# Decode attention with its gradients: scores of chunk pairs through four 32-column array tiles, a first load moved ahead, and another row order for one weight

## The chip, the core and the metric

The kernel runs on one core of one Trainium2 chip. The metric is the time on the device in microseconds (us); the median of a kernel's runs is quoted.

## What is computed

One decode step of an attention layer plus a gated MLP, forward and all gradients, in bf16. The caches of 32 heads hold 8192 positions of 128 values each; there is one query.

```python
def _A_ref(x, k_cache, v_cache, wq, wo):              # x: [1, 1, 640]; k_cache, v_cache: [1, 32, 8192, 128]
    q = (x @ wq).reshape(B, Sq, Hq, Dh) ...
    scores = jnp.einsum("bhqd,bhkd->bhqk", q, k) * (Dh ** -0.5)
    p = softmax(scores)
    o = jnp.einsum("bhqk,bhkd->bhqd", p, v)
    return o.reshape(B, Sq, Hq * Dh) @ wo
def _B_ref(x, w1, w3, w2):                            # w1, w3: [640, 1728]; w2: [1728, 640]
    return (silu(x @ w1) * (x @ w3)) @ w2
out = x + _A_ref(layernorm(x), ...) + _B_ref(layernorm(x), ...)
# outputs: out, and the gradients of x, k_cache, v_cache, wq, wo, w1, w3, w2 for a given grad_out
```

The gradient of the K cache is an outer product per head (a weight per position times q), that of the V cache another (the probabilities times dO, the gradient of the head's output). So each head loads K and V, 2 MB each, and stores dK and dV, 2 MB each: 64 loads and 64 stores of 2 MB make up 134 MB each of the 151.67 MB read and the 151.34 MB written.

## The kernel before

Positions lie on the 128 partitions, 64 per partition. A ring of ten slots of 2 MB holds the caches; a head's gradients are written over its caches and stored from the same slot, and when the store has been issued the next load waits for a slot to become free. The MLP runs once, just before head 2, in four of the ten slots. The parts that matter here (cuts marked):

```python
    load_group(0, nc.sync)                     # wq and wo of the first four heads, rows of 1 KB and 1280 B
    for _ in range(4):
        load_next()                            # K0, V0, K1, V1
    # ... slots for the MLP; w2a is 12 blocks of 128 rows of w2
    fifo(w2a, B_w2[0:NBA * P, :].rearrange("(fb p) c -> p fb c", p=P))      # pieces of 1280 B
    # ...
    def T(h, kind, c):                         # one of eight chunks of a head's K or V
        W3 = kv_tiles[(kind, h)][:].bitcast(F32)...            # a pair of bf16 is moved as one fp32
        pT = pst()                             # one of four PSUM tiles
        for k in range(4):
            nc.tensor.transpose(pT[:, k * P:(k + 1) * P], W3[:, 4 * c + k, :], ident_f[:])
        KT = kt_tile()                         # one of four copy tiles in SBUF
        nc.scalar.copy(KT..., pT[:])
    def M(h, kind, c):                         # scores (K) or V*dO (V) of the chunk: 8 matmuls
        # ...
        for k in range(4):
            for par in range(2):
                nc.tensor.matmul(S_[kind][:, 0:J], lhsT=KTb[:, k, par, :], rhs=S_["cz"][:, o:o + J], ...)   # J = 64
    def wsum(h, kind, pair):                   # weighted sum over the positions, in four column tiles
        nc.tensor.matmul(X[:], lhsT=zeros, rhs=W[:, 0:N4], start=True, ...)     # clears the tile
        for i in range(J // 4):
            q = QW * (i % 4)                   # QW = 32
            nc.tensor.matmul(X[q:q + 4, :], lhsT=pair[:, 4 * i:4 * i + 4, 0], rhs=W[:, N4 * i:N4 * (i + 1)], ...)
        nc.scalar.copy(XS..., X[:])
    # ... MLP
            nc.tensor.matmul(gu_ps[0:rows, wi, b:b + 1], lhsT=wrow(wi, ci)[:, b * P:b * P + rows], ...)
            # ...
            nc.scalar.copy(bc_sb[:, wi, f0:f1], pb[:, 0:f1 - f0])
    # ... after a head's dK: store("K", h), which issues the store and then load_next()
```

A head has two long products per cache on VectorE (the gradients), 16 chunks of transposes with 16 copies on ScalarE, 128 score matmuls and four groups of small sums on TensorE.

## Time and profile before

| | before |
|---|---|
| time, median of the runs beside the changed kernel (six) | 743.96 us (743.29 to 746.13) |
| bytes moved over the span | 304.3 MB in 743.1 us |
| TensorE, VectorE, ScalarE busy | 82%, 60%, 50% |
| a head that never waits for a load, from row maximum to row maximum | 17.6 to 18.1 us |
| a head on average (heads 3 to 31) | 20.69 us |

Lines of the page. The row "DMA" is the busy share of the 16 DMA engines in 40 slices of the span, in tenths; "GB/s" what they moved. A group line reads: line, engine, operation, output<-input, shapes, count | busy us, mean ns | idle time of the engine before it, and what ended most of that.

```profile
span 743.1 us, 20151 instructions
...
PE 607.7 (82%) x8767; PEld 512.8 (69%) x8767; DVE 447.5 (60%) x740; ACT 370.9 (50%) x732; POOL 30.4 (4%) x45
...
DMA  8999999999999999999999999999999999999992
GB/s 320 384 408 419 422 425 428 352 428 421 406 424 431 425 423 427 426 427 426 424 428 426 428 426 425 426 427 426 424 427 426 420 424 423 418 423 421 421 404 92
...
q8 instruction: 69, 1.13, 0.6%
...
DMA 61%; PE 28%; DVE 6%; issue 1%; ACT 1%; SPq 0%; DVEq 0%; ACTq 0%
...
L279 PE MATMUL pT<-ident_f,kv 128*128 128x128 f32 x2048 | 338.9, 291 | 73.9 <-DMA kv<-in_A_k_cache_dram 65.4
...
L298 PE MATMUL dA<-cz,KT 128*128 128x64 bf16 x2048 | 107.7, 197 | 6.6 <-ACT qd L315 4.5
L298 PE MATMUL sA<-cz,KT 128*128 128x64 bf16 x2048 | 102.8, 193 | 0.0
...
L321 DVE TENSOR_REDUCE mrow<-sA 128x1 f32<-128x64 f32 x32 | 7.2, 224 | 60.1 <-PE sA L298 60.1
...
```

What to see: the DMA row is full from the second slice to the last but one, mostly at about 425 GB/s; the chain that ended last is 61% DMA; TensorE's one large idle time, 73.9 us before the transposes of line 279, ended with a K load 65.4 us of the time. The score matmuls of line 298 keep TensorE busy for 107.7 + 102.8 = 210.5 us, but that is hidden: compute waits for transfers. Two blemishes stand in the GB/s row: the eighth slice (352) and the two ends.

The ends, in a table of stretches (start:end, length, then busy us and instructions per engine, granted clock, DMA share, GB/s):

```profile
...
core 0: us, PE busy (x) PEld busy (x) DVE busy (x) ACT busy (x) POOL busy (x), PEclk, DMA share, GB/s
0.00:5.00 5.00, 0.00 (x0) 0.00 (x0) 1.76 (x13) 1.28 (x1) 0.69 (x6) 1.00 0.49 76
...
130.00:150.00 20.00, 19.70 (x313) 17.38 (x311) 14.18 (x20) 12.97 (x26) 0.76 (x1) 1.00 0.93 357
200.00:690.00 490.00, 418.78 (x5964) 353.65 (x5964) 291.73 (x451) 260.82 (x515) 16.31 (x20) 0.92 1.01 425
...
```

In the first 5 us only 76 GB/s flowed; in 130 to 150 us the DMA share was 0.93. The transfers of the last 55 us, in 40 slices of 1.375 us, look like this:

```profile
...
GB/s 441 426 444 432 417 417 441 411 429 441 393 298 477 405 411 334 381 429 405 417 465 429 417 359 407 278 365 267 141 18 30 30 18 27 36 24 24 12 0 0
...
```

Read the last third of that row. Up to about 730 us the engines move hundreds of GB/s. Then nine slices carry 12 to 36 GB/s. All 16 engines together move about 425, so one engine is worth some 27: in these 12 us one engine is finishing alone. The page alone hides it, since the DMA share is a mean of 16. I call it the straggler.

### The profile page before, as it was taken

What the parts mean: (1) busy time and instruction counts of PE and PEld (TensorE: products, weight loads), DVE (VectorE), ACT (ScalarE), POOL (GpSimd) and SP (SyncE); (2) the same over time, 40 slices, a digit from 0 to 9 for tenths busy, and PEclk for the clock granted to TensorE, in tenths of its full rate; (3) what the DMA queues carried; (4) which work ended last, traced back from release to release, by engine and by line L of the source; (5) the groups of instructions that cost most, each with busy time, mean ns of one, the idle gap of its engine ahead of it and who ended that gap; (6) DMA issues with size and microseconds to landing.
All of it is one profiled execution on the core that took longest, in us unless ns stands there. A gap on an engine that the chain in (4) does not pass through costs nothing.

```text
span 743.1 us, 20151 instructions
## 1 busy us (share of the span) xinstructions
PE 607.7 (82%) x8767; PEld 512.8 (69%) x8767; DVE 447.5 (60%) x740; ACT 370.9 (50%) x732; POOL 30.4 (4%) x45
## 2 busy tenths in 40 slices
PE   1997699999998969878797997889698788888920
PEld 1776588888886867767586775767687677777710
DVE  4169927677764745666366664547546666476580
ACT  1651076666664646545365553556455455555510
POOL 0100200000000000001000000000000000000000
PEclk9997799999998999999899998989989999899965
DMA  8999999999999999999999999999999999999992
GB/s 320 384 408 419 422 425 428 352 428 421 406 424 431 425 423 427 426 427 426 424 428 426 428 426 425 426 427 426 424 427 426 420 424 423 418 423 421 421 404 92
DMA packets 29118, 304.32 MB, mean 410 GB/s; under 512 B 2836, under 2 KB 5972, under 8 KB 12644
## 3 DMA queue, kind: packets, MB, share of 16 engines
q1 hardware_dynamic: 22736, 276.39, 88.5%
q0 software_dynamic: 5984, 26.30, 8.8%
q8 instruction: 69, 1.13, 0.6%
q10 hardware_dynamic: 308, 0.33, 0.2%
q14 instruction: 21, 0.17, 0.1%
HBM read 151.67 MB, written 151.34 MB: 408 GB/s over the span
## 4 chain that ended last, share of the span: by engine, by line
DMA 61%; PE 28%; DVE 6%; issue 1%; ACT 1%; SPq 0%; DVEq 0%; ACTq 0%
DMA kv<-in_A_k_cache_dram 27%; DMA out_dram<-kv 26%; PE pT L279 12%; DMA kv<-in_A_v_cache_dram 8%; PE pT L365 3%; PE sA L298 3%; PE dA L298 3%; DVE kv L398 3%; PE hb L391 2%; PE pT L361 1%; PE dh_ps L481 1%; PE hb L377 1%; PE acc L555 1%; PE sA L325 1%; DVE kv L558 1%
## 5 line engine op out<-in xcount | busy, mean ns | idle before, releaser
L281 ACT COPY KT<-pT 128x512 f32<-128x512 f32 x512 | 299.1, 586 | 213.8 <-PE pT L279 187.4
L279 PE MATMUL pT<-ident_f,kv 128*128 128x128 f32 x2048 | 338.9, 291 | 73.9 <-DMA kv<-in_A_k_cache_dram 65.4
L279 PEld LDWEIGHTS pT<-ident_f,kv 128*128 128x128 f32 x2048 | 234.5, 150 | 77.8 <-issue 75.7
L298 PEld LDWEIGHTS <-KT 128*128 128x128 bf16 x4096 | 194.7, 100 | 28.3 <-issue 21.4
L398 DVE TENSOR_TENSOR kv<-qd,U 128x4096 bf16<-128x4096 bf16 x64 | 146.0, 2283 | 0.0
L398 DVE TENSOR_TENSOR kv<-qd,P 128x4096 bf16<-128x4096 bf16 x64 | 143.4, 2282 | 0.0
L298 PE MATMUL dA<-cz,KT 128*128 128x64 bf16 x2048 | 107.7, 197 | 6.6 <-ACT qd L315 4.5
L298 PE MATMUL sA<-cz,KT 128*128 128x64 bf16 x2048 | 102.8, 193 | 0.0
L368 ACT COPY KT<-pT 128x512 f32<-128x512 f32 x64 | 37.5, 586 | 74.0 <-PE pT L365 45.9
L354 DVE SCALAR_TENSOR_TENSOR U<-dA,P 128x64 bf16<-128x64 f32 x32 | 7.4, 232 | 97.1 <-PE dA L298 97.1
L391 PE MATMUL hb<-masks,KT 128*128 128x1 f32 x512 | 65.8, 250 | 0.0
L391 PEld LDWEIGHTS hb<-masks,KT 128*128 128x128 f32 x512 | 62.0, 192 | 0.9 <-issue 0.9
L321 DVE TENSOR_REDUCE mrow<-sA 128x1 f32<-128x64 f32 x32 | 7.2, 224 | 60.1 <-PE sA L298 60.1
L379 DVE SCALAR_TENSOR_TENSOR U<-dA,hb,P 128x128 bf16<-128x128 f32 x32 | 11.4, 355 | 51.0 <-PE hb L377 51.0
L365 PE MATMUL pT<-kv,P 128*4 128x512 bf16 x512 | 41.6, 455 | 0.0
L365 PE MATMUL pT<-kv,U 128*4 128x512 bf16 x512 | 33.1, 379 | 0.4 <-DVE U L379 0.4
L361 PE MATMUL pT<-kv,cz 128*128 128x512 bf16 x64 | 27.6, 432 | 0.0
L448 DVE SCALAR_TENSOR_TENSOR wq_g<-wq_g,side 128x512 bf16<-128x512 bf16 x40 | 27.3, 682 | 0.0
L345 DVE RECIPROCAL rZ<-sA 128x1 f32<-128x1 f32 x32 | 5.4, 168 | 35.7 <-PE sA L339 34.8
L238 DVE SCALAR_TENSOR_TENSOR side<-wo_g,g_bc 128x640 bf16<-128x640 bf16 x32 | 26.1, 817 | 0.3
L365 PEld LDWEIGHTS <-P 128*4 128x4 bf16 x512 | 10.3, 90 | 22.1 <-issue 12.7
L377 PEld LDWEIGHTS hb<-rdot,masks 128*128 128x128 f32 x64 | 11.0, 216 | 17.8 <-issue 17.8
(140 smaller groups left out, 344.7 us busy)
## 6 DMA issues: line engine op xcount, KB each, us to landing
out_dram<-kv SPq DMA_DIRECT2D x64, 2048.0 KB, 31.5
kv<-in_A_k_cache_dram SPq DMA_DIRECT2D x32, 2048.0 KB, 26.7
kv<-in_A_v_cache_dram SPq DMA_DIRECT2D x32, 2048.0 KB, 26.6
out_dram<-wo_g POOLq DMA_DIRECT2D x8, 640.0 KB, 12.2
out_dram<-wq_g POOLq DMA_DIRECT2D x8, 640.0 KB, 13.7
wq_g<-in_A_wq_dram POOLq DMA_DIRECT2D x7, 640.0 KB, 13.7
wo_g<-in_A_wo_dram POOLq DMA_DIRECT2D x7, 640.0 KB, 19.4
kv<-in_B_w_dram SPq DMA_DIRECT2D x2, 1728.0 KB, 16.8
```

Of the source, the lines that this page charges most:

```text
L238: nc.vector.scalar_tensor_tensor(junk[:], G_["wo"][:, hh, :], 1.0, g_bc[:], ALU.mult, ALU.mult, accum_out=G_["do"][:, hh:hh + 1])
L279: nc.tensor.transpose(pT[:, k * P:(k + 1) * P], W3[:, 4 * c + k, :], ident_f[:])
L281: nc.scalar.copy(KT[:].rearrange("p k w -> p (k w)"), pT[:])
L298: nc.tensor.matmul(S_[kind][:, 0:J], lhsT=KTb[:, k, par, :], rhs=S_["cz"][:, o:o + J], start=(i == 0 and par == 0), stop=(par == 1), skip_ ...
L361: nc.tensor.matmul(X[:], lhsT=cz_tiles[0][:, 0:1].to_broadcast([P, P]), rhs=W[:, 0:N4], start=True, stop=False, skip_group_check=True)
L365: nc.tensor.matmul(X[q:q + 4, :], lhsT=pair[:, 4 * i:4 * i + 4, 0], rhs=W[:, N4 * i:N4 * (i + 1)], start=False, stop=(i >= J // 4 - 4), sk ...
L368: nc.scalar.copy(XS[:].rearrange("p k w -> p (k w)"), X[:])
L377: nc.tensor.matmul(S_["hb"][:, 2:3], lhsT=negones_b, rhs=S_["rdot"][:], start=True, stop=True, skip_group_check=True)
L379: nc.vector.scalar_tensor_tensor(S_["U2"][:], S_["V"][:, 0:J].unsqueeze(2).to_broadcast([P, J, 2]), S_["hb"][:, 2:3], S_["P2"][:], ALU.add ...
L391: nc.tensor.matmul(S_["hb"][:, a:a + 1], lhsT=XS[:, r, :], rhs=mask4[:, r:r + 1], start=False, stop=(r == 3), skip_group_check=True)
L398: nc.vector.tensor_tensor(dst[:, lo * DH:hi * DH].rearrange("p (j a b) -> p j a b", a=DH // 2, b=2), vec.rearrange("p (a b) -> p a b", b=2 ...
L448: nc.vector.scalar_tensor_tensor(wq_g[:, ci, :], wq_g[:, ci, :], 1.0, dqb, ALU.mult, ALU.mult, accum_out=dxa[:, ci, g:g + 1])
```

## The change

The intent is to take work off TensorE and to use the transfers better at the start and around the MLP. In scores and V*dO, the chunk was the stationary operand (128 columns) and a 64-column strip moved past it: 8 matmuls per chunk. Now the query strip is stationary (32 columns) and 512 columns of the chunk move; two chunks, each split into even and odd positions, go through four column tiles of the array, so four matmuls serve a pair. The result lies in rows and is turned to columns by a copy and four fp32 matmuls against a 0/1 matrix ("selection"). With it the clearing matmul of the weighted sums goes, K0 is loaded first, w2 is laid out with twelve consecutive rows per partition (15 KB pieces), and the two last small stores are split.

```diff
+    load_next()
     load_group(0, nc.sync)
-    for _ in range(4):
+    for _ in range(3):
         load_next()
...
-    fifo(w2a, B_w2[0:NBA * P, :].rearrange("(fb p) c -> p fb c", p=P))
+    fifo(w2a, B_w2[0:NBA * P, :].rearrange("(p fb) c -> p fb c", fb=NBA))
...
-    def M(h, kind, c):
+    def Mp(h, kind, c0):
...
+        for c in (c0, c0 + 1):
+            KTb = ...
+            for par in range(2):
+                q = QW * (2 * (c - c0) + par)
+                o = QL + QW * (2 * a + par) - c0
+                nc.tensor.matmul(S_[kind][q:q + QW, :], lhsT=S_["qz"][:, o:o + QW], rhs=KTb[:, par, :],
+                                 start=(c0 == 0), stop=(c0 == NCH - 2), skip_group_check=True)
+    def ev(h, kind):
+        XS = kt_tile()
+        nc.scalar.copy(XS[:].rearrange("p k w -> p (k w)"), S_.pop(kind)[:])
+    def selm(h, kind):
         for k in range(4):
-            for par in range(2):
-                nc.tensor.matmul(S_[kind][:, 0:J], lhsT=KTb[:, k, par, :], rhs=S_["cz"][:, o:o + J], ...)
+            nc.tensor.matmul(S_["m"][:, b0:b0 + J]...[:, k, :, :], lhsT=XS[:, k, :], rhs=selc[:]..., ...)
...
     def wsum(h, kind, pair):
-        nc.tensor.matmul(X[:], lhsT=cz_tiles[0][:, 0:1].to_broadcast([P, P]), rhs=W[:, 0:N4], start=True, ...)
...
-                nc.tensor.matmul(gu_ps[0:rows, wi, b:b + 1], lhsT=wrow(wi, ci)[:, b * P:b * P + rows],
+                nc.tensor.matmul(gu_ps[0:rows, wi, b:b + 1], lhsT=fcols(wrow(wi, ci), b, rows),     # every 12th column
...
+                if b0 < NBA:
+                    nc.scalar.copy(bc_sb[:, wi, 0:NBA * P].rearrange("p (f b) -> p b f", b=NBA)[:, b0:b0 + bn, :], ...)
+                    continue
...
-    nc.scalar.dma_start(out_0..., fin_bf[0:NC, :])
-    nc.scalar.dma_start(out_1..., fin_bf[NC:2 * NC, :])
+    for dst, r0, cuts in ((out_0, 0, (0, 3, 5)), (out_1, NC, (0, 4, 5))):
+        for lo, hi in zip(cuts, cuts[1:]):
+            nc.scalar.dma_start(dst...[lo:hi, :], fin_bf[r0 + lo:r0 + hi, :])
```

Left out: the order of the calls in a head, which now treats chunks by pairs; the small sums of a head, which share one PSUM tile ("m") with the turned scores; padding of the probability tiles, with which the weights of each weighted-sum matmul become 32 columns wide instead of 4.

## The prediction

> **What bounds the kernel now.** DMA, and within it one engine. The page counts 304.3 MB over 743.1 us. In the table of stretches the DMA share is 1.0 at 415 to 433 GB/s in almost every 10 us from 10 to 700 us; by the packet records no engine idles except at 0-7 us, 130-148 us (about 1.4 us per engine) and after 700 us. Tensor is 82% busy, but a head that runs freely takes 17.8 us (106.7 to 124.8 to 142.4 us in the chain of waits), its transfers about 20.6 us: compute is hidden.
>
> The end is set by a straggler. The last compute ends at 727 us, fifteen engines finish near 730, yet packets of one engine run on, back to back, until 742 us. In the landings of each 2 MB transfer the sixteenth increment trails the fifteenth by 0.1 us at 190 us, 4 at 390, 9 at 640, 12 to 14 at the end. My reading: instruction fetch. Queue 8 moved 69 packets of 16 KB, 1.01 us each; 17,534 Tensor instructions at 64 B make 68.5 such packets. The Trainium skill, "Runtime: NRT & Kernel Launch", "Instruction fetch mechanics", says instructions are refilled in 16 KiB blocks (256 instructions) by a DMA queue of the sequencer; this trace agrees. The spread between engines at the end (17 to 19 us) fits one engine taking a third of the fetches.
>
> **What the change does.**
> 1. Score matmuls: 4096 of 64 columns become 1024 of 512 in four column tiles. The weighted sums, tiled so already, take 60 ns each (16 in 0.96 us), so a pair of chunks costs about 0.25 instead of 0.8 us. Added: 512 passes of fp32 selection (8 in 0.87 us, as the column sums) and two 0.59 us ScalarE copies per head; 64 zeroing matmuls (0.43 us) go. About -3.5 us of Tensor and +1.2 us of ScalarE per head. Directly worth nothing: off the critical path.
> 2. Tensor instructions fall to about 12,290: 48 fetches instead of 69. With a third on the straggler: about -5.5 us.
> 3. K0 first: from 1 to 7 us the engines moved 0.94 MB in 1 KB pieces where 2.5 MB were possible. 16 KB pieces first hide that: -2 to -3 us. Compute starts about 6 us earlier.
> 4. The hole at 130-148 us comes from late stores after the MLP; earlier, faster heads mostly fill it: -1 us.
> 5. w2a in 15 KB rows instead of 1280 B (61 ns each): -1.3 us. Strided weight loads in the MLP hide under VectorE.
> 6. Split last stores: one of five descriptors sat on the straggler (landing 3.5 to 4.5 us after the others), but the last cache store lands later there: 0.
>
> Sum about -10.5 us. **Predicted 733.5 us, 80% range 728 to 739.** Faster by over 2%: 0.20; within: 0.78; slower: 0.02.
>
> **What would show it.** Queue 8 near 48 packets; DMA share still 1.0 in the plateau; Tensor busy near 500 us, idling more for K and V loads; ScalarE near 405 us; higher GB/s in the first slices and in slice 8 (352 before); lag at the end about 8 us; some 700 packets of 1280 B on queue 1 instead of 2240.
>
> **What would make it wrong.** The straggler has another cause than fetches (about 738); it vanishes and the end falls to the compute tail after the last V load (727 to 730); the ring of copy tiles, now shared by selection, makes a head longer than 20.6 us (slower); Tensor time matters where I call it hidden.

## The result

The changed kernel took 737.50 us (736.41 to 739.99, six runs), the kernel before 743.96 us in the same rounds. The ratio is 0.9914, with a 95% interval of 0.9892 to 0.9936: within 2%, and in the predicted range (728 to 739). The gain is about 6.5 us where 10.5 were predicted. A ratio is computed as the mean time of one kernel's undisturbed runs over that of the other's in the same rounds, so it is not quite the ratio of the medians quoted. All outputs are correct.

The same lines of the page, after:

```profile
span 735.9 us, 14854 instructions
...
PE 639.8 (87%) x6143; PEld 464.7 (63%) x6143; DVE 446.7 (61%) x745; ACT 402.5 (55%) x796; POOL 29.9 (4%) x45
...
DMA  9999999999999999999999999999999999999993
GB/s 338 401 409 421 425 430 423 391 413 410 428 420 423 428 427 426 417 426 428 430 417 425 430 427 426 419 431 425 427 419 427 428 428 429 425 429 429 424 391 150
...
q8 instruction: 48, 0.79, 0.4%
...
PE 64%; DMA 12%; DVE 10%; ACT 8%; issue 3%; ACTq 0%; SPq 0%; DVEq 0%
...
L293 PE MATMUL pT<-ident_f,kv 128*128 128x128 f32 x2048 | 311.3, 291 | 5.9 <-DMA kv<-in_A_k_cache_dram 4.0
...
L328 PE MATMUL m<-selc,KT 128*128 128x16 f32 x512 | 68.0, 265 | 29.3 <-ACT KT L318 29.2
...
L354 DVE TENSOR_REDUCE mrow<-m 128x1 f32<-128x64 f32 x32 | 7.2, 225 | 106.4 <-PE m L328 106.4
...
L312 PE MATMUL sA<-KT,qz 128*32 128x512 bf16 x512 | 56.0, 427 | 0.0
...
L312 PE MATMUL dA<-KT,qz 128*32 128x512 bf16 x512 | 53.6, 404 | 0.2 <-ACT KT L295 0.2
...
```

Instructions fell from 20,151 to 14,854, queue 8 from 69 packets to 48, as predicted, and the score matmuls (line 312 now) are busy for 56.0 + 53.6 = 109.6 us, half of the 210.5 before. What was not predicted: TensorE's busy time rose, from 607.7 to 639.8 us, and the chain that ended last is now 64% TensorE and 12% DMA. The transposes (line 293 now) wait 5.9 us for anything before them, where they waited 73.9. A kernel that waited for transfers now hardly waits. The reason isn't faster transfers: the DMA row is as full as before. The heads have grown by about as much as they used to wait. (The ends of matmuls are modelled in this profile, so the time of a head, below, is a better measure than busy time.) The row maximum shows a longer way within a head: VectorE sat idle before it for 106.4 us in all, 60.1 before; the scores now pass through ScalarE and once more through TensorE (lines 318 and 328) on their way there. The stretches, with the columns as before:

```profile
...
0.00:5.00 5.00, 0.00 (x0) 0.00 (x0) 1.76 (x13) 1.28 (x1) 0.69 (x6) 1.00 0.65 198
...
130.00:150.00 20.00, 18.86 (x187) 13.82 (x186) 12.28 (x18) 11.86 (x25) 0.00 (x0) 0.91 0.99 391
200.00:690.00 490.00, 457.43 (x4370) 328.83 (x4370) 312.26 (x476) 291.76 (x595) 17.95 (x22) 0.94 1.01 426
...
```

The first 5 us carry 198 GB/s, 130 to 150 us carry 391. Over the long plateau from 200 to 690 us, TensorE is busy 457 of 490 us (419 before) and the rate is 426 GB/s (425 before). The end:

```profile
...
GB/s 417 465 441 393 441 453 322 274 322 429 393 435 381 357 381 405 489 429 393 417 405 399 273 367 284 115 24 27 33 30 18 36 0 0 0 0 0 0 0 0
...
```

Six slices, 8 us, below 40 GB/s, where before there were nine.

The heads can be told apart by the reduction in which VectorE takes the row maximum of the scores, one per head:

| us | before | after |
|---|---|---|
| head 1 to head 2, with the MLP between | 55.4 | 63.5 |
| head 2's row maximum at | 100.0 | 111.5 |
| a head that doesn't wait for loads | 17.6 to 18.1 | 19.0 to 20.8 |
| a head, mean of heads 3 to 31 | 20.69 | 20.16 |
| last row maximum at | 700.0 | 696.1 |

### A ledger of DMA engine time

Each DMA packet in the trace has a start, a duration, a size and a queue. Summed and divided by 16, they give the time per engine that transfers took; "idle" is the time in which fewer than 16 packets were under way, times the share of engines missing. (Packet records overlap a little, so the columns add up to some 6 us more than the span, 6.6 before and 6.1 after.) This is worked out from the packet records for the profiled execution of every kernel below (us per engine). "Data" is the time of all packets but the instruction queue's; "fetch" that of the instruction queue; "last" the idle time from 680 us to the end of the last transfer, which is large only if some engine runs on while the others have finished; the two last columns are the part of "data" by which 16 KB packets exceeded their usual 611 ns, from 100 to 200 us and from 400 to 700 us.

| kernel | span | data | fetch | idle 0-20 | idle 20-150 | last | slow 100-200 | slow 400-700 |
|---|---|---|---|---|---|---|---|---|
| before | 743.1 | 725.9 | 4.37 | 2.99 | 1.37 | 13.60 | 2.95 | 3.25 |
| after | 735.9 | 723.9 | 3.09 | 2.28 | 0.08 | 11.46 | 3.36 | 1.75 |
| change | -7.2 | -2.0 | -1.3 | -0.7 | -1.3 | -2.1 | +0.4 | -1.5 |

The five middle entries of the last line add up to -7.4, about the change of the span (-7.2). So the gain is the straggler's end (-2.1), fetches as such (-1.3), the hole around 130 us (-1.3), the start (-0.7), and data (-2.0, of which the pieces of w2, loaded and stored, -1.1).

My theory at this point was the prediction's: fewer instruction fetches are the main gain, and the other parts add to it. The rival: fetches are worth nothing, since only 69 packets of 1 us are spread over 16 engines, and reading packets of the straggler back from the end (each packet's record begins 3 or 4 ns before the end of the one ahead of it) gave it no fetch packet before and one after; but such a chain can be followed only a short way, in the kernel before to about 718 us. Then the gain would come from the start, w2 and the hole. A second question: which part of the expected gain was lost, and where.

### The profile page after: what moved, and what is told of

It reads as the page before. It is cut to its first block, busy times and chain, and to the rows that moved or that the text cites. A ratio compares the mean times of both kernels' runs of the same rounds, so it can differ in the third digit from the quotient of the medians. Undisturbed runs are those within 1.5% of the kernel's fastest.

```text
span 735.9 us, 14854 instructions
## 1 busy us (share of the span) xinstructions
PE 639.8 (87%) x6143; PEld 464.7 (63%) x6143; DVE 446.7 (61%) x745; ACT 402.5 (55%) x796; POOL 29.9 (4%) x45
## 4 chain that ended last, share of the span: by engine, by line
PE 64%; DMA 12%; DVE 10%; ACT 8%; issue 3%; ACTq 0%; SPq 0%; DVEq 0%
PE pT L293 27%; PE m L328 8%; PE m L423 7%; DMA kv<-in_A_k_cache_dram 7%; PE sA L312 6%; PE pT L398 5%; ACT KT L295 4%; DVE kv L430 4%; DMA kv<-in_A_v_cache_dram 4%; PE dA L312 2%; DVE side L239 2%; ACT KT L318 2%; DMA wo_g<-in_A_wo_dram 2%; PE gu_ps L507 1%; PE m L372 1%
## 5 line engine op out<-in xcount | busy, mean ns | idle before, releaser
L293 PE MATMUL pT<-ident_f,kv 128*128 128x128 f32 x2048 | 311.3, 291 | 5.9 <-DMA kv<-in_A_k_cache_dram 4.0
L293 PEld LDWEIGHTS pT<-ident_f,kv 128*128 128x128 f32 x2048 | 245.8, 153 | 49.8 <-PE pT L293 17.5
L328 PEld LDWEIGHTS m<-selc,KT 128*128 128x128 f32 x512 | 62.3, 192 | 49.5 <-ACT KT L318 44.8
L328 PE MATMUL m<-selc,KT 128*128 128x16 f32 x512 | 68.0, 265 | 29.3 <-ACT KT L318 29.2
L423 PEld LDWEIGHTS m<-masks,KT 128*128 128x128 f32 x512 | 65.0, 200 | 15.4 <-issue 15.4
L354 DVE TENSOR_REDUCE mrow<-m 128x1 f32<-128x64 f32 x32 | 7.2, 225 | 106.4 <-PE m L328 106.4
L423 PE MATMUL m<-masks,KT 128*128 128x1 f32 x512 | 70.2, 259 | 0.0
L312 PE MATMUL sA<-KT,qz 128*32 128x512 bf16 x512 | 56.0, 427 | 0.0
L312 PE MATMUL dA<-KT,qz 128*32 128x512 bf16 x512 | 53.6, 404 | 0.2 <-ACT KT L295 0.2
L312 PEld LDWEIGHTS <-qz 128*32 128x32 bf16 x1024 | 26.6, 93 | 41.4 <-issue 40.3
L398 PE MATMUL pT<-kv,U 128*32 128x512 bf16 x512 | 46.2, 497 | 0.9 <-DVE U L411 0.9
L398 PE MATMUL pT<-kv,P 128*32 128x512 bf16 x512 | 34.7, 387 | 0.0
## 6 DMA issues: line engine op xcount, KB each, us to landing
out_dram<-kv SPq DMA_DIRECT2D x64, 2048.0 KB, 28.8
```

Source lines behind the costliest of these rows:

```text
L312: nc.tensor.matmul(S_[kind][q:q + QW, :], lhsT=S_["qz"][:, o:o + QW], rhs=KTb[:, par, :], start=(c0 == 0), stop=(c0 == NCH - 2), skip_grou ...
L328: nc.tensor.matmul(S_["m"][:, b0:b0 + J].rearrange("p (c k t) -> p k c t", k=4, t=2)[:, k, :, :], lhsT=XS[:, k, :], rhs=selc[:].rearrange( ...
L398: nc.tensor.matmul(X[q:q + QW, :], lhsT=pair[:, 4 * i:4 * i + QW, 0], rhs=W[:, N4 * i:N4 * (i + 1)], start=(i < 4), stop=(i >= J // 4 - 4) ...
L423: nc.tensor.matmul(S_["m"][:, OC + a:OC + a + 1], lhsT=XS[:, r, :], rhs=mask4[:, r:r + 1], start=False, stop=(r == 3), skip_group_check=True)
```

## The experiments

All ran with the kernel before beside them on the same chip. "One part alone" is the kernel before with that part of the diff.

### K0 first, alone

```diff
+    load_next()
     load_group(0, nc.sync)
-    for _ in range(4):
+    for _ in range(3):
```

> The kernel before with the first K load moved ahead of the first weight loads, nothing else. My theory (the start of the DMA stream is slow because the first pieces are 1 KB): 2 to 3 us faster than before, ratio 0.996 to 0.997, and the rate of the first 5 us rises from 76 GB/s to about 200. Rival (the end is set by the straggling DMA engine, which makes up a late start out of later idle time): no difference, ratio 1.000.

Measured: 742.89 us against 744.69, ratio 0.998 (0.9966 to 0.9993): -1.5 us. The rate of the first 5 us rose from 76 to 201 GB/s, as expected, and idle time in the first 20 us fell from 2.99 to 2.31. Worth something, but less than the 2 to 3 us predicted.

### The row order of w2, alone

```diff
-    fifo(w2a, B_w2[0:NBA * P, :].rearrange("(fb p) c -> p fb c", p=P))
+    fifo(w2a, B_w2[0:NBA * P, :].rearrange("(p fb) c -> p fb c", fb=NBA))
... (with fcols, the strided ScalarE copy and the store of the gradient, as in the change)
```

> The kernel before with w2 loaded and stored as contiguous rows per partition, and the strided weight loads and broadcast copies that this needs. My theory: the packet time saved on all 16 engines is 1.1 us each (725.9 to 723.9 us per engine was measured for the whole change, of which w2 makes 1.1), so 1 us faster, ratio 0.998 to 0.999. Rival (the strided work makes the MLP longer and the hole in the DMA stream after it deeper): 2 us or more slower, ratio over 1.002.

Measured: 741.93 us, ratio 0.9967 (0.9955 to 0.998): -2.4 us, more than the packets alone (1.1 us). In the ledger the idle time of 20 to 150 us went from 1.37 to 0 and the slow packets of 100 to 200 us from 2.95 to 0.57. So this part alone also closes the hole that the prediction had left to faster heads. The MLP stretch did grow, from 55.4 to 61.9 us, as the rival had it; but the heads after it, at 17.6 us, are shorter than their transfers, and here the longer MLP cost no time that the gain did not cover.

### All but the attention

```diff
... (K0 first, the row order of w2 and the split last stores; M, wsum and head() as before)
```

> The kernel before with K0 first, w2 by rows, and the split last stores, but with the old score matmuls. If the restructured scores are worth nothing because compute is hidden: as fast as the changed kernel, ratio 0.991 to 0.993. If fewer Tensor instructions (fewer instruction fetches) give a third to a half of the gain, as predicted: 0.994 to 0.997. Queue 8 shows 69 packets.

Measured: 741.05 us, ratio 0.9958 (0.9944 to 0.9971): -3.1 us. Queue 8 had 68 packets. The MLP stretch was 59.4 us long (55.4 before). The end of the transfers is still the long one (GB/s in slices of 1.375 us from 690 us, as above): after a slice of 72, eight slices carry between 12 and 36 GB/s.

```profile
...
GB/s 435 405 429 441 429 393 471 381 262 214 250 393 405 399 393 369 417 381 405 360 448 453 343 425 325 240 72 33 30 18 27 36 24 24 12 0 0 0 0 0
...
```

### The attention alone

```diff
... (M -> Mp, ev, selm, wsum without the clearing matmul, head() by pairs; K0, w2 and the last stores as before)
```

> The changed scores, selection and weighted sums alone, with the old order of loads, the old w2 layout and the old last stores. Prediction on record (fetches): 4 to 5 us faster, ratio 0.993 to 0.995. Rival from the traces (the straggler carries no fetch, its lag of 18.5 us against the fastest engine at 690 us is the same in both kernels): ratio 0.998 to 1.000; if the longer heads of the changed kernel (19.9 us running free, against 17.8) cost something, up to 1.003. Queue 8 shows 48 packets.

Measured: 737.68 us, ratio 0.9914 (0.99 to 0.9928): -6.4 us, as much as the whole change. Queue 8 had 48 packets. The end, in the same view:

```profile
...
GB/s 453 441 405 429 441 357 310 286 310 238 357 429 423 405 203 405 500 405 405 393 489 405 342 299 282 304 39 27 30 30 18 21 0 0 0 0 0 0 0 0
...
```

Six thin slices, as after. The ledger (before, then this kernel): fetch 4.37 to 3.10, last 13.60 to 11.22, slow packets from 400 to 700 us 3.25 to 1.83; idle 20 to 150 us 1.37 to 0.01, slow packets from 100 to 200 us 2.95 to 1.21. The rival's number (0.998 to 1.000) falls: nothing of K0, w2 or the last stores is in this kernel. But the hole closed here too, and two things are mixed, fewer instructions and another shape of the heads; the next pair separates these two.

The three single parts sum to -10.3 us (-1.5, -2.4, -6.4), close to the predicted -10.5. Together they give -6.4 us. That is the main finding about the size: the parts don't add.

### More instructions, or the same TensorE time in fewer

Both in the kernel before, in each head but two: matmuls with a throwaway result into a free part of a PSUM tile, ahead of the last products of the head before.

```diff
-        S_["hb"] = ps_h.tile([P, 4], F32, name="hb", tag="hb")
+        S_["hb"] = ps_h.tile([P, 512], F32, name="hb", tag="hb")
...
         if has_prev:
+            for _ in range(80):                                  # narrow: 80 of 1 column; wide: 13 of 504
+                nc.tensor.matmul(hd[h - 1]["hb"][:, 8:9], lhsT=ident_bf[:], rhs=g_bc[:, 0:1], start=False, stop=True, ...)
             outers_b(h - 1)
```

> The kernel before with 80 extra matmuls of one column per head from head 1 on (head 2 left out), result never read: about 4,800 more Tensor instructions, so some 87 fetch packets on queue 8 instead of 69, and about 2.9 us more Tensor time per head, which its slack (17.8 of 20.6 us) just covers. Theory on record (fetches delay the end, a third of them on the straggler): 5 to 7 us slower, ratio 1.007 to 1.010. Fetches spread evenly over the engines: 1.2 us slower, ratio 1.001 to 1.002. The pair to compare it with is the wide kernel below, which has the same Tensor time in few instructions.

> The kernel before with 13 extra matmuls of 504 columns per head instead: about the same extra Tensor time, only 780 more instructions, queue 8 at about 72 packets. If instruction bytes matter and Tensor time does not: ratio 1.000 to 1.001, clearly below the narrow kernel. If what matters is how long a head keeps the Tensor engine busy (longer heads spread the transfers otherwise, as the changed kernel's heads of 19.9 us do): different from 1.000, and equal to the narrow kernel; it could even be faster than before.

Lines of the page of the profile, of the narrow kernel and then of the wide one: TensorE's busy time, the instruction queue, and the added matmuls.

```profile
...
PE 669.2 (90%) x11165; PEld 583.4 (78%) x11167; DVE 447.9 (60%) x740; ACT 371.3 (50%) x732; POOL 30.5 (4%) x45
...
q8 instruction: 87, 1.43, 0.7%
...
L672 PE MATMUL hb<-g_bc,ident_bf 128*128 128x1 bf16 x2400 | 64.3, 163 | 0.0
...
```

```profile
...
PE 660.9 (89%) x9155; PEld 532.8 (72%) x9157; DVE 448.4 (60%) x740; ACT 369.6 (50%) x732; POOL 30.5 (4%) x45
...
q8 instruction: 71, 1.16, 0.6%
...
L672 PE MATMUL hb<-g_bc,ident_bf 128*128 128x504 bf16 x390 | 87.7, 375 | 0.0
...
```

Measured: narrow 748.24 us, ratio 1.0047 (1.0029 to 1.0065); wide 745.68 us, ratio 1.0009 (0.9992 to 1.0027); the kernel before 743.97. Both load TensorE about equally (669.2 and 660.9 us busy, against 607.7), and in both the transposes still wait for transfers (18.3 and 23.8 us in all); only the one with many more instructions is slower than the kernel before. Between the two there are 16 packets of instructions and 0.38%, 2.8 us: about 0.18 us per packet. The intervals of the two don't overlap. The granted clock (0.914 in the narrow kernel's profile, 0.966 in the wide one's) is no explanation, since the kernel before had 0.915. And the heads of the wide kernel that don't wait, 19.6 to 20.8 us, are as long as those of the changed kernel, yet it is not faster than the kernel before: longer heads by themselves are not where the gain comes from. The 0.18 us is more than a packet's own share: at about 1 us of one engine, it is 0.06 us per engine. In the ledger the rest shows as slower 16 KB packets (from 400 to 700 us 6.95 in narrow, 3.99 in wide, 3.25 before) and a later last engine (14.30, 13.35, 13.60).

So more instructions cost time here; that it is their bytes, and not their number, is the likely reading, and no run sets the two apart. 21 fewer packets at 0.18 us are worth 3.8 us (an estimate from these two runs). The ledger of the attention alone gives 5.1 for fetch, last and the late slow packets together (1.3, 2.4 and 1.4). The prediction had 5.5.

### Relief for one engine

If the straggler sets the end, and it is one of the first engines, taking bytes off it should help. The Trainium skill, "DMA: Bandwidth & Descriptors", section "Why a DMA increments its semaphore by 16 and not by 1", says that a transfer runs on the largest number of engines up to 16 that divides the slowest dimension, and, where these are fewer, on the lowest-numbered (for hardware queues, as this store's). One store of 2 MB was cut in two, of 92 and 36 partitions: by that rule 92 go to four engines.

```diff
+        if kind == "K" and h == 12:
+            fifo(dst[0:92], t[0:92])
+            fifo(dst[92:P], t[92:P])
+        else:
+            fifo(dst, t[:])
```

> The changed kernel with one store of 2 MB (K gradient of head 12) cut at partition 92: 92 rows of 16 KB go over four engines (23 each), 36 over twelve (3 each). By the Trainium skill (DMA: Bandwidth & Descriptors, how many engines) these are the lowest-numbered ones. The straggler took its descriptor of the five-way last store late in the kernel before and of none in the four-way one, so I take it for the fifth engine: its load falls by 5 rows of 0.61 us. If it sets the end: 2.5 to 3.5 us faster than the changed kernel, ratio to before 0.987 to 0.989. If the straggler is not that engine or the end is set by computing: 0.991, or worse if the four loaded engines are not among those that lag least.

Measured: 739.15 to 759.08 us, median 743.13; two of the six runs took 759 us, and the profile fell into one of these, so it can't be compared. The four shorter runs give 0.9962 (0.9936 to 0.9987), worse than the changed kernel without the cut (0.9914). The relief failed. The trace still shows that the count by the rule holds here: after a first update at the issue, the completion semaphore of the 92 rows rose four times (366.3 to 373.8 us), that of the 36 rows twelve times (351.6 to 376.4). Which engines these were, and which engine is late, stays open. With this one uneven cut in 64 stores the times lie up to 20 us apart; why, no run here shows.

### How near compute is to the limit

The wide matmuls in the changed kernel:

```diff
         if has_prev:
+            scr = pst()
+            for _ in range(13):
+                nc.tensor.matmul(scr[:, 0:504], lhsT=ident_bf[:], rhs=g_bc[:, 0:504], start=True, stop=True, ...)
             outers_b(h - 1)
```

> The changed kernel with the 13 extra wide matmuls per head. If its heads of 19.9 us have used up the slack against 20.6 to 21.2 us of transfers: 1.4 to 2.4 us per head too long, 30 heads, so 30 to 60 us slower, ratio 1.03 to 1.08, with the Tensor engine never waiting for a load. If the Tensor engine's time is still hidden, as the prediction had it (some 14 us per head): ratio 0.99.

Measured: 744.55 us, ratio 0.9996 (0.9975 to 1.0018) to the kernel before, so some 6 us above the changed kernel. I had expected far more; a head grew only from 20.16 to 20.53 us on average, because the added matmuls filled times in which TensorE waited: its 29.2 us of waits for ScalarE ahead of the selection fell to 0.5. But the last row maximum came at 709.1 us instead of 696.1, and two lines of the page, the chain that ended last and the transposes, show the state that this kernel is in:

```profile
...
PE 81%; ACT 10%; DVE 4%; issue 3%; DMA 2%; SPq 0%; ACTq 0%; DVEq 0%
...
L293 PE MATMUL pT<-ident_f,kv 128*128 128x128 f32 x2048 | 298.2, 282 | 0.0
...
```

The transposes never wait for a load, and the chain that ended last is 81% TensorE. In the kernel before, the same matmuls cost nothing measurable (0.09%). That is the slack that the change has used up.

### K0 first and the attention, without the row order of w2

```diff
... (the changed kernel with w2, fcols, the copies of the MLP and the last stores as before)
```

> The changed scores with K0 first, but the old w2 layout and old last stores. My theory now: with the w2 rows the strided ScalarE copies in the MLP (6 of 2.3 us) make the MLP 8 us longer (mean stretch from the second to the third head's maximum 63.5 us against 55.3 with the old layout), and with heads of 20 us the kernel cannot make this up, so the transfers run thin at 100 to 200 us, which eats what w2 rows and K0 first gain. Expect: MLP stretch about 55 us, slow 16 KB packets at 100 to 200 us at about 1.2 instead of 3.4 us per engine, time 1 us under the changed kernel: ratio 0.989 to 0.991. Rival (K0 first is worth nothing with the new scores): same as the attention change alone, 0.9914 or above.

Measured: 737.89 us against 744.54, ratio 0.9905 (0.989 to 0.992). The MLP stretch is 57.5 us (63.5 in the changed kernel), and the slow packets of 100 to 200 us take 1.64 (3.36). So with the new heads, the row order of w2 is worth nothing that these runs show: the likely reading is that what it saves in packets comes back as a longer MLP. (The split of the last stores is missing here too.)

### The row order made by TensorE, not by a strided copy

Where the row order costs was read from the trace. First the copy to bc_sb in the kernel before (six of 128x512, among others), then in the changed kernel, where its output steps by 24 bytes: the durations, and who waited for it.

```profile
...
L544 ACT CAST kv<-pT 128x512 bf16<-128x512 f32 x6 | 3.2, 620 | 3.8 <-PE pT L539 3.8
...
```

```profile
...
L580 ACT CAST kv<-pT x6: 2427/2738/2799, 79.8 to 91.0; 128x512 bf16<-128x512 f32 x6
...
  PE pT L576: 5.3, 3
  DVE KT L593: 3.9, 1
...
```

From 0.62 to between 2.43 and 2.80 us. The skill's page "SBUF — State Buffer", section "Door 1: The DMA port swizzle", says that SBUF has lines of 16 bytes and that each access crossing to a new line pays; steps of 24 bytes do so every time, and this trace agrees in direction. The gate and up matmuls, whose weights are now every twelfth column, also slowed: 140 weight loads of 104 ns (median) became 161 ns, and the group took 8.3 us, not 4.2.

```diff
-                if b0 < NBA:
-                    nc.scalar.copy(bc_sb[...strided...], pb[...])
+            for n in range(4):
+                pb = pst()
+                for b in range(NBA):               # 12 matmuls of 32 columns, written every 12th column of PSUM
+                    nc.tensor.matmul(pb[:, 0:W4].rearrange("p (f b) -> p b f", b=NBA)[:, b, :],
+                                     lhsT=dgu_bf[:, wi, b:b + 1].to_broadcast([P, P]),
+                                     rhs=ident_bf[:, n * QW:(n + 1) * QW], start=True, stop=True, ...)
+                nc.scalar.copy(bc_sb[:, wi, n * W4:(n + 1) * W4], pb[:, 0:W4])
```

> The changed kernel, but the row order of the broadcast gradients in the MLP made by the Tensor engine (48 matmuls of 32 columns with strided PSUM output per weight), so that the ScalarE copies are contiguous (0.45 us instead of 2.3 us). Theory: MLP stretch from 63.5 to about 56 us, slow packets at 100 to 200 us from 3.4 to about 1.2 us per engine, 2 to 2.5 us faster than the changed kernel: ratio to before 0.987 to 0.989. Rival (the end is set by instruction fetch and the straggler alone, the thin stretch is made up later): 0.991.

The same copies, in the groups by form:

```profile
...
L580 ACT CAST kv<-pT 128x384 bf16<-128x384 f32 x8 | 3.6, 482 | 4.6 <-PE pT L576 4.3
...
```

Measured: 736.96 us, ratio 0.9891 (0.9877 to 0.9906). A copy (128x384 now) takes 0.48 us, the MLP stretch 59.7 us, the slow packets of 100 to 200 us 1.02. This bears the mechanism out: plain copies take 3.8 us off the MLP, and most of the slow packets go. The gain over the changed kernel, 0.9891 to 0.9914, lies within the intervals, so it is likely but not shown. The MLP is still 4 us longer than before, and 2 us longer than with the new heads and the old row order (57.5); the strided weight loads (4 us more) remain.

### A copy of the head moved off the path

Where a head's time goes now, in the timeline of the changed kernel (start, length, engine and line; in brackets the idle time before and what ended it):

```profile
...
start us, us, engine line op out<-in xcount [idle before <-releaser]
315.07 2.28 DVE L430 TENSOR_TENSOR kv<-qd,U 128x4096 bf16<-128x4096 bf16 x1
...
317.21 0.41 PE L312 MATMUL dA<-KT,qz 128*32 128x512 bf16 x4
...
317.44 0.37 ACT L348 CAST qd<-pT 128x256 bf16<-128x256 f32 x1 [0.92 <-DVE kv L430]
317.45 1.03 PE L398 MATMUL pT<-kv,P 128*32 128x512 bf16 x16
317.71 1.08 ACT L295 COPY KT<-pT 128x512 f32<-128x512 f32 x2
...
318.66 0.62 ACT L318 COPY KT<-dA 128x512 f32<-128x512 f32 x1
...
319.14 0.63 ACT L401 COPY KT<-pT 128x512 f32<-128x512 f32 x1
...
319.33 1.07 PE L328 MATMUL m<-selc,KT 128*128 128x16 f32 x8 [0.85 <-ACT KT L318]
...
```

VectorE's long product (2.28 us) began at 315.07 and ended at 317.35. ScalarE had waited 0.92 us for it, to write q and dO of the next head (line 348). Only then came two chunk copies, and only then, at 318.66, the copy of the scores of V (line 318), whose matmuls had run by 317.62. TensorE waited 0.85 us for it ahead of the selection (line 328). One copy that nobody needs yet holds up the one that the head waits for. The edit moves it behind:

```diff
             rows_pe(h + 1, pst()[:, 0:2 * DH], True)
-            rows_act(h + 1)
...
         o_sum(h)
+        if nxt:
+            rows_act(h + 1)
         selm(h, "V")
```

> As the one before, and the ScalarE copy of the next head's rows moved behind the copies that the end of a head waits for (it waits up to 1.6 us for VectorE and holds back the V*dO selection). Theory: free-running heads fall from 20.15 us to 18.5 to 19.2 us, so Tensor waits for loads again in the second half; slow packets at 100 to 300 us fall below 1 us per 100 us; the time falls by 0 to 1.5 us against the run before: ratio 0.986 to 0.989. Rival (the longer heads do no harm, or even keep the transfers in a better order, as late slow packets were fewer with them): equal to it, or slower by up to 1 us.

The chain that ended last and the transposes, from the page of this kernel:

```profile
...
PE 47%; DMA 39%; DVE 5%; ACT 5%; issue 2%; SPq 0%; ACTq 0%; DVEq 0%
...
L293 PE MATMUL pT<-ident_f,kv 128*128 128x128 f32 x2048 | 321.6, 297 | 30.8 <-DMA kv<-in_A_k_cache_dram 21.8
...
```

Measured (with the plain copies of the MLP): 736.49 us, ratio 0.9888 (0.9871 to 0.9904). Heads that don't wait take 17.5 to 18.9 us instead of 19.0 to 20.7, TensorE's idle time ahead of the selection falls from 28.8 to 1.8 us, and the transposes again wait for loads, 30.8 us in all. So the order on ScalarE was worth some 1.5 to 1.9 us per head. The slow packets of 100 to 200 us did not fall below 1 us as expected (1.89). In time it is worth 0.5 us over the version without it, which is nothing that these runs can tell from noise: once a head is under the 20 to 21 us of its transfers, its length doesn't matter, as the prediction had said. This version is the fastest tried, and beats the kernel before by 1.1%; over the changed kernel it is about 1 us ahead, and the intervals overlap.

## Why the prediction was right or wrong

**The time fell within 2% and in the range, as predicted**; the sum was 4 us too good. That the time fell in the range was in part luck: a term that went the wrong way, the time of a head, stayed just short of costing time, and 737.5 us is also what the prediction named for the case that fetches are not the straggler's cause (about 738). Only the runs tell these apart. By its numbered terms:

1. *"About -3.5 us of Tensor"* per head: wrong. A head that runs freely went from about 17.8 us to 19.0 to 20.8, not to some 14 (17.8 less 3.5). The first mis-sized term was *"a pair of chunks costs about 0.25"* us: it was scaled from 16 matmuls in a row (0.96 us), but four alone take 0.41 us, which makes 1.3 us in the eight pairs of a head. A cost paid once per group fits both: by these two numbers, each further matmul costs about 0.05 us and the first some 0.27 (an estimate). The skill's page "TensorEngine Tiling (Array Packing)", section "Performance Considerations", warns that tiling speeds up TensorE but not the evacuation of PSUM; this trace agrees only at first sight: TensorE waits 29.2 us for the copies of line 318 ahead of the selection, but the last experiment moved one ScalarE copy out of their way and all but 1.8 us of that wait went. That order was worth 1.5 to 1.9 us of a head. Even so a head stayed at 17.5 to 18.9 us; what keeps it from 14 was not taken apart. The longer way of the scores to the row maximum (VectorE's 106.4 us of waiting, 60.1 before) is a part that the prediction left out: it counted a head as TensorE time, and a head is a chain over three engines. *"Directly worth nothing: off the critical path"* was nearly right for the time, but with little to spare: the heads stopped, with 20.16 us on average, just short of the 20.6 us that the prediction named as the limit (*"makes a head longer than 20.6 us (slower)"*).
2. *"48 fetches instead of 69 [...] about -5.5 us"*: the count was exact, the size about right (3.8 by the pair of narrow and wide, 5.1 by the ledger of the attention alone). *"With a third on the straggler"* was not confirmed, and the narrow kernel speaks against it: of its 18 packets more than before a third, 6 of 1 us, would have put some 6 us on one engine (an estimate), but "last" grew from 13.60 to 14.30 only. The gain shows in three places: fetch time on all engines, the last engine, and slower packets late in the run. How a fetch makes other packets and one engine later is not settled.
3. *"K0 first: [...] -2 to -3 us"*: -1.5 alone, and 0.7 of idle time in the ledger of the whole change. The first transposes did begin 4.4 us earlier (at 11.0 us, 15.4 before), but the first row maximum did not come earlier (27.7 us, 26.4 before).
4. The hole *"-1 us"*: idle 1.4 us per engine and, with it, slow packets of up to 2.4 us, which the prediction hadn't seen. That *"earlier, faster heads mostly fill it"* failed in its reason: heads weren't faster, and the row order of w2 alone filled it too. Why the attention part fills it with longer heads, no run shows.
5. w2 in long rows, *"-1.3 us"*: packets -1.1, and -2.4 alone because it closes the hole as well. **The step that failed is the sentence after it: "Strided weight loads in the MLP hide under VectorE."** They don't, with the old heads or the new: this part made the MLP stretch longer in both, from 55.4 to 61.9 us alone and from 57.5 to 63.5 us with the new heads. The group of matmuls with the strided loads took twice as long, the strided copies four times as long, and VectorE waited 3.9 us for one of these. What differs is what follows: heads of 17.6 us catch up on transfers of some 20.6 us per head, heads of 19.0 to 20.8 hardly do. So alone the part gained 2.4 us, and in the whole change nothing of it can be seen (0.9905 without it, 0.9914 with it). The prediction named the strided loads and overlooked the strided copy.
6. The split last stores, 0: as predicted. The pieces land together now, but a cache store still lands last.

**And the sum itself.** The single parts measured -1.5, -2.4 and -6.4 us; the terms, though individually off, summed to about the same -10.5. The ledger shows why the whole gives only -6.5 (us per engine, one profile of each kernel; a "w2" with the plain copies is the version with the row order made by TensorE):

| kernel | data | fetch | idle 0-20 | idle 20-150 | last | slow 100-200 | MLP stretch |
|---|---|---|---|---|---|---|---|
| before | 725.9 | 4.37 | 2.99 | 1.37 | 13.60 | 2.95 | 55.4 |
| all but the attention | 723.3 | 4.28 | 2.25 | 0.01 | 13.94 | 0.60 | 59.4 |
| the attention alone | 723.7 | 3.10 | 2.63 | 0.01 | 11.22 | 1.21 | 55.3 |
| attention and K0 | 724.0 | 3.11 | 2.33 | 0.02 | 11.88 | 1.64 | 57.5 |
| after | 723.9 | 3.09 | 2.28 | 0.08 | 11.46 | 3.36 | 63.5 |
| after, plain copies | 722.0 | 3.12 | 2.32 | 0.00 | 12.30 | 1.02 | 59.7 |

First, overlap: the hole (1.4 us of idle time) and the slow packets around it (1.7 to 2.4 us) are closed by the w2 part and by the attention part, each alone, and can be closed only once. Second, giving back: from the attention alone to the whole change, "data" doesn't fall (723.7 to 723.9), though the pieces of w2 save 1.1 us; the slow packets of 100 to 200 us grow by 2.2, beside an MLP that is 8 us longer. With the plain copies "data" falls to 722.0. So about 3 us count twice in the sum of the parts, and the gain of w2 was, by this reading, lost to the MLP. The two last versions win back about 1 us, which the intervals don't set apart from zero; and in the very last the slow packets were 1.89, so a part of this column varies with other things.

Of what the prediction said would show it: queue 8 near 48, yes; DMA share in the plateau, yes; the lag at the end near 8 us, yes; ScalarE near 405 us, yes (402.5); higher GB/s in the first slices and slice 8, yes (338 and 391, from 320 and 352); some 700 packets of 1280 B on queue 1, yes (704). TensorE near 500 us and waiting more for loads: the opposite (639.8 us, waiting less), and this was the sign that a step had failed, though the time fell in the range.

Open: which engine is late and what slows its loads; whether and how instruction fetches delay it; the two groups of times of the uneven cut.

## What to carry to other kernels

When transfers are saturated, look at the tail of each DMA engine and not at the mean share, and count instruction fetches as traffic: fewer, larger instructions can pay even where the engine that runs them is hidden. Terms that fill the same hole must not be added; run each part alone and look for the same column falling twice. Changing a row order to lengthen DMA pieces moves the stride to an engine, so cost every reader and writer of the new order, and cost a short group of matmuls by itself, not by the rate of a long one. Time saved on a hidden engine, or added to it, is free only within the slack: know how much of it a change uses up.

## What the Trainium skill lacked or had wrong

- "Runtime: NRT & Kernel Launch", section "Instruction fetch mechanics", calls the cost of a 16 KiB boundary mostly hidden. The block size agrees (17,534 TensorE instructions made 69 packets, 12,286 made 48). The cost was not hidden here, where DMA is saturated: 16 more packets went with 2.8 us, 0.18 us each.
- "DMA: Bandwidth & Descriptors", section "Latency and other measured facts", names engines 7 and 15 as usually slower, for transfers with descriptor rings in SBUF. Here one engine ends some 12 us after all others (before) and 8 us (after), mostly on transfers of a hardware queue; I found no page that tells of a single late engine that falls back over the whole run.
- The same page has the rule for uneven splits (used above), and the count agrees (four landings for 92 rows, twelve for 36), but not that six runs of one program with one such cut among 64 stores came out at 739 to 744 us and twice at 759.
- "TensorEngine Tiling (Array Packing)" gives up to 4x for 32 columns and about 60 cycles per matmul, but not what a short group costs: four tiles of 512 columns took 0.41 us, one burst of 16 took 0.96.
- "SBUF — State Buffer", section "Door 1: The DMA port swizzle", has the 16-byte lines, but no figure for a ScalarE copy: 128x512 bf16 went from 0.62 us to 2.43 to 2.80 at a step of 24 bytes.
